# Raw rows and rounded pairs fetched in two tiles each, the first fetches reordered, the last output tiles copied in halves, under a new plan

## Chip, cores and metric

The kernel runs on one core of a Trainium2 chip. The metric is the device time of one execution in microseconds. The kernel before has a median of 574.6 us over three runs (574.01 to 575.79).

## What is computed

Two layers in sequence, for 8 batches of 576 positions: local attention with 8 heads of 64 (a window of 128 and a linear bias), and on its output a mixture of 4 attention experts of which each position uses the best two.

```python
def _attn_ref(q, k, v):
    ...
    scores = scale * np.matmul(q, k.transpose(0, 1, 3, 2))
    ...
    mask = (rel >= 0) & (rel < window)
    scores = np.where(mask, scores + bias[None], -1000000000.0)
    ...
    attn = attn / (np.sum(attn, axis=-1, keepdims=True) + 1e-09)
    return np.matmul(attn, v).astype(np.float32)

def _moe_ref(x, w_gate, wq, wk, wv, wo):
    ...
    logits = x @ w_gate
    topk = np.argpartition(-logits, K, axis=-1)[..., :K]
    ...
    for e in range(E):
        q = x @ wq[e]
        k = x @ wk[e]
        v = x @ wv[e]
        scores = scale * (q @ k.transpose(0, 2, 1))
        causal = np.triu(np.ones((S, S), dtype=bool), 1)
        ...
        ye = a @ v @ wo[e]
        for kk in range(K):
            mask = topk[:, :, kk] == e
            out += mask[..., None] * w[:, :, kk:kk + 1] * ye
    return out.astype(np.float32)
```

## The kernel before

The attention works on 32 groups, a pair of heads of one batch each (`g`, four to a batch). Group `g` goes through scores (`attn_s`: matmuls into tile `s`, mask and bias on VectorE, exponentials on ScalarE into `p`, scaling by 1/sum on GpSimd or ScalarE), transposition by TensorE (`attn_t`, tiles `t`, `pa`) and the product with the values (`attn_pv`, tiles `x`, `xt`, result `xh`, `xl`). After four groups of a batch come its projections (`qkproj`, `vproj`), the experts' scores (`moe_s`, tile `ms`), their transposition (`mt`), the product with the values (`ma`, `mal`) and the output (`moe_wo`, tile `o`, copied to `ot` and stored).

Precise products of f32 numbers are made of rounded ones: a high part and the rest are multiplied apart. For a group the rounded q and k of both heads stand in one tile `h` (two head halves side by side, each with q and a tail of zeros or of the other head, then k), which a DMA on GpSimd's queue fetches and rounds. The raw numbers stand in one tile `r` (q, then k), fetched on SP's queue; `prep` subtracts the rounded from the raw: `q0` and `q1` into `h` itself, `k0` and `k1` into `klA`. There is one buffer of `r`, two of `h`. The first six groups (`N32`) don't use this form: their raw rows, tile `e`, are multiplied as f32; `load_e` fetches the lower 64 partitions on SP and the upper ones on ScalarE's queue (groups 0 to 3) or GpSimd's (groups 4 and 5).

The weights of the projections come in four chunks (`wload`, tile `wst`), are rounded on GpSimd or ScalarE (`wprep`: `WH`) and their rests (`WL`) computed on VectorE or GpSimd. `wo` and the mask table follow.

The order in which instructions stand on each engine is neither the program's nor written by hand: all operations are recorded, and `plan` sorts them by a list schedule. It takes costs of each operation, the longest chain behind it as its rank, offsets of the rank by tile, engine and phase (`off`, 193 numbers in the table `K`), rates for fetches (`dr`), and where an operation may go to one of two engines (`nc.any`), it chooses one. Where TensorE has nothing to do in the plan up to 69.6 us (`f1`), it puts in a matmul of zeros (`warm`, into a tile that nobody reads). Then each engine executes its instructions in that order. SP's and ScalarE's fetches share eight semaphores, so each one waits for the landing of the eighth before it.

Of the kernel before, what the change touches and what calls it, by code (L numbers as in the profile page):

```python
# [417 lines left out]
def attn_moe_kernel(ctx, tc, hd, rd, vd, wall, wo, mk, tb, tm, mt, ident, out):  # L418
# [73 lines left out]
    HW = 2 * QW + 2 * S  # L492
# [8 lines left out]
    def load_e(g):  # L501
        b, p = divmod(g, NP_)
        o1 = QW + S + P
        if g < NP_:
            e = m1.tile([P, 10 * P], F32, tag="mp", name=f"e{g}", bufs=K["mp"])[:, : QW + S]
        else:
            e = p2.tile([P, HW], F32, tag="h", name=f"e{g}")
            for x in range(3):
                nc.alt["hold"][len(nc.ops) + x] = first["w", 1]
            nc.sync.dma_start(e[:, QW + S : o1], hd[b, p, :, QW + S : o1])  # L510
        nc.sync.dma_start(e[:D, : QW + S], hd[b, p, :D, : QW + S])
        q = nc.scalar if g < NP_ else nc.gpsimd
        q.dma_start(e[D:, P : QW + S], hd[b, p, D:, o1 + P : o1 + QW + S])
        raws[g] = e
# [24 lines left out]
    def load_hi(g):  # L539
# [6 lines left out]
        h = p2.tile([P, HW], F32R, tag="h", name=f"h{g}")  # L546
        hh = [h[:, :o1], h[:, o1:]]
# [760 lines left out]
```

## Time and profile before

| | before |
|---|---|
| median of 3 runs | 574.6 us (574.01 to 575.79) |
| profiled execution, its own time | 577.87 us |
| span of the profiled execution | 575.9 us |
| mean granted TensorE clock | 0.996 |
| busy VectorE | 418.0 us (73%) |
| HBM read, written | 65.32 MB, 9.44 MB |

The profile shows one execution. PE is TensorE's matmuls, PEld its weight loads, DVE VectorE, ACT ScalarE, POOL GpSimd; SPq, ACTq and POOLq are the queues on which DMAs are issued. "Idle before" a group is the time in which its engine stood, with what ended it behind the arrow. Every recorded operation is issued from one line (L1220), so instructions are told apart by the tiles that they write and read: `s<-e` writes `s` and reads `e`. Matmuls overlap in the array, so a busy PE may still have small gaps between starts.

### The profile page before, as it was taken

How to read it: one execution, taken by the hardware profiler on the slowest of the kernel's cores; microseconds unless marked ns; L12 is line 12 of the kernel's file. 1: busy time of each engine (PE TensorE's matmuls, PEld its weight loads, DVE VectorE, ACT ScalarE, POOL GpSimd, SP SyncE). 2: the span in 40 equal slices, each digit the busy share in tenths (PEclk: the TensorE clock that was granted, in tenths of full speed). 3: DMA queues.
4: the chain of work that ended last, by engine and by line, in shares of the span. 5: the costliest groups of instructions: out<-in, count | busy, mean ns of one | idle time of the engine just before them, and what ended most of it. 6: DMA issues, size and time to landing. Idle time of an engine off the chain costs nothing.

```text
span 575.9 us, 13867 instructions
## 1 busy us (share of the span) xinstructions
PE 558.8 (97%) x4576; PEld 476.7 (83%) x4576; DVE 418.0 (73%) x1818; ACT 427.6 (74%) x1458; POOL 364.1 (63%) x570
## 2 busy tenths in 40 slices
PE   8799999999999999989999999999999999999996
PEld 7577978888888988979888898888888898898764
DVE  3778779977977789676977689766997668465620
ACT  3776778977797688876888687876789768475863
POOL 3575578686768587675878478695768744063430
PEclk9999999999999999999999999999999999999999
DMA  9934454344452435523453444504455400100013
GB/s 217 304 109 134 153 187 140 129 152 152 170 188 65 148 111 207 189 86 116 160 194 125 136 158 179 207 20 151 153 187 171 147 24 24 73 20 2 1 56 109
DMA packets 24246, 75.64 MB, mean 131 GB/s; under 512 B 2416, under 2 KB 3952, under 8 KB 24176
## 3 DMA queue, kind: packets, MB, share of 16 engines
q1 hardware_dynamic: 16624, 40.72, 22.0%
q0 software_dynamic: 7232, 32.93, 17.5%
q10 hardware_dynamic: 320, 1.11, 0.9%
q8 instruction: 36, 0.59, 0.4%
q14 instruction: 34, 0.28, 0.2%
HBM read 65.32 MB, written 9.44 MB: 130 GB/s over the span
## 4 chain that ended last, share of the span: by engine, by line
PE 74%; DVE 6%; POOL 4%; DMA 4%; ACT 3%; issue 1%; ACTq 0%; POOLq 0%
PE qk L1220 15%; PE s L1220 9%; PE v L1220 8%; PE o L1220 8%; PE ms L1220 6%; PE x L1220 6%; PE mt L1220 6%; PE ma L1220 5%; PE t L1220 5%; DMA r<-in_rd 2%; PE msl L1220 2%; POOL h L1220 2%; DMA h<-in_hd 2%; ACT p L1220 1%; PE mal L1220 1%
## 5 line engine op out<-in xcount | busy, mean ns | idle before, releaser
L1220 ACT ACTIVATE p<-p,nm 128x128 f32<-128x128 f32 x288 | 113.1, 394 | 39.9 <-DVE nm L1220 37.2
L1220 PE MATMUL qk<-xh,WH 128*128 128x288 f32 x512 | 115.4, 308 | 0.0
L1220 POOL TENSOR_TENSOR h<-r,h 64x576 fp32r<-64x576 f32 x52 | 74.0, 1423 | 43.9 <-DMA h<-in_hd 24.3
L1220 POOL TENSOR_SCALAR mp<-mp,mr,w 128x128 f32<-128x128 f32 (+3 forms) x128 | 76.6, 611 | 31.3 <-DVE mr L1220 24.4
L1220 PEld LDWEIGHTS qk<-xh,WH 128*128 128x128 f32 x512 | 82.4, 189 | 5.2 <-issue 1.1
L1220 ACT ACTIVATE mp<-mp,mnm 128x384 f32<-128x384 f32 (+3 forms) x128 | 71.3, 559 | 12.2 <-DVE mnm L1220 10.9
L1220 POOL TENSOR_SCALAR p<-p,r 128x128 f32<-128x128 f32 x156 | 57.2, 380 | 35.7 <-DVE r L1220 29.5
L1220 DVE TENSOR_TENSOR pa<-t,tmt 128x512 f32<-128x512 f32 (+2 forms) x96 | 73.8, 774 | 7.3 <-ACT pa L1220 4.4
L1220 DVE CUSTOM_DVE_ANT_0 mp<-ms,mtt 128x384 f32<-128x384 f32 (+3 forms) x128 | 59.9, 486 | 21.5 <-PE ms L1220 19.9
L1220 POOL TENSOR_TENSOR klA<-r,h 64x576 fp32r<-64x576 f32 x52 | 73.9, 1421 | 2.2
L1220 DVE CUSTOM_DVE_ANT_0 p<-s,tbt 128x128 f32<-128x128 f32 x288 | 71.3, 285 | 2.7 <-PE t L1220 0.8
L1220 PE MATMUL qk<-xh,WL 128*128 128x288 f32 x256 | 71.3, 307 | 0.0
L1220 PE MATMUL s<-h 128*128 128x128 f32 (+2 forms) x260 | 69.2, 286 | 1.9 <-DVE nm L1220 1.9
L1220 PE MATMUL s<-klA,h 128*128 128x128 f32 (+2 forms) x260 | 69.6, 284 | 1.3 <-POOL klA L1220 1.3
L1220 DVE COPY_PREDICATED s<-mkt,s 128x256 f32<-128x256 int32 (+2 forms) x160 | 51.4, 331 | 26.2 <-PE s L1220 24.6
L1220 PE MATMUL v<-WH,xh 128*128 128x260 f32 x288 | 63.1, 298 | 0.1
L1220 PE MATMUL x<-pa,vt 128*64 128x256 f32 (+1 forms) x512 | 62.7, 361 | 0.0
L1220 PE MATMUL t<-idt,p 128*128 128x128 f32 x288 | 56.4, 278 | 5.3 <-ACT p L1220 3.5
L1220 PE MATMUL mt<-idt,mp 128*128 128x128 f32 x320 | 59.2, 274 | 0.1
L1220 ACT COPY mpt<-mt 128x384 f32<-128x384 f32 (+1 forms) x86 | 45.4, 535 | 17.6 <-PE mt L1220 14.1
L1220 ACT ACTIVATION_READ_ACCUMULATOR p<-p,nm 128x1 f32 x288 | 54.2, 188 | 0.0
L1220 PEld LDWEIGHTS s<-h 128*128 128x128 f32 x260 | 48.8, 189 | 5.1 <-issue 2.6
(128 smaller groups left out, 1405.7 us busy)
## 6 DMA issues: line engine op xcount, KB each, us to landing
h<-in_hd POOLq DMA_DIRECT2D x26, 1216.0 KB, 6.6
r<-in_rd SPq DMA_DIRECT2D x26, 576.0 KB, 3.8
vt<-in_vd SPq DMA_DIRECT2D x32, 320.0 KB, 3.0
out<-ot SPq DMA_DIRECT2D x32, 256.0 KB, 2.0
e<-in_hd SPq DMA_DIRECT2D x6, 304.0 KB, 7.8
wst<-in_wall SPq DMA_DIRECT2D x4, 386.0 KB, 6.5
e<-in_hd ACTq DMA_DIRECT2D x4, 272.0 KB, 6.1
out<-ot SPq DMA_DIRECT2D x8, 128.0 KB, 2.4
```

What stands on the lines that cost most here:

```text
L1220: getattr(getattr(tc.nc, e), m)(*a, **k)
```

## The change

`r` becomes `rq` and `rk` (q rows and k rows) with a fetch each, `h` becomes `ha` and `hb` (head 0, head 1) with a fetch each; groups 4 and 5 keep raw rows in `ea` and their tails in `eb`. GpSimd's queue takes the upper halves of groups 1 to 3 from ScalarE's, the second and third of them behind memsets. SP's first fetches stand in another order. The last two output tiles of the last batch are copied half by ScalarE and half by VectorE, and each half is stored by its own queue. All offsets and a few constants of the plan are new: `dr`, the rate of fetches that the planner reckons with in the first 30 us, is 300 in place of 340.

```diff
-K = {'dx': 1200, 'se': 0, 'hd': 1, 'dr': 340, 
...
+K = {'dx': 1200, 'se': 0, 'hd': 1, 'dr': 300, 
...
-            e = p2.tile([P, HW], F32, tag="h", name=f"e{g}")
+            e = p2.tile([P, QW + S], F32, tag="ha", name=f"ea{g}")
+            eb = p2.tile([P, QW + S], F32, tag="hb", name=f"eb{g}")
...
-        q = nc.scalar if g < NP_ else nc.gpsimd
+        if 0 < g < NP_:
+            nc.alt["hold"][len(nc.ops)] = first["z", min(g, 2)]
+        q = nc.gpsimd if g else nc.scalar
...
-            r = raw.tile([P, 2 * S], F32, tag="r", name=f"r{g}")
-            if g < N32 + 2:
-                nc.alt["hold"][len(nc.ops)] = first["w", 1]
-            nc.sync.dma_start(r, rd[b, p])
+            r = [raw.tile([P, S], F32, tag="r" + x, name=f"r{x}{g}") for x in "qk"]
+            for k in range(2):
+                if g < N32 + 2:
+                    nc.alt["hold"][len(nc.ops)] = first["w", 1]
+                nc.sync.dma_start(r[k], rd[b, p, :, S * k : S * k + S])
...
-        h = p2.tile([P, HW], F32R, tag="h", name=f"h{g}")
-        hh = [h[:, :o1], h[:, o1:]]
+        hh = [p2.tile([P, o1], F32R, tag="h" + "ab"[k], name=f"h{'ab'[k]}{g}") for k in range(2)]
...
-        if g < N32 + 2:
-            nc.alt["hold"][len(nc.ops)] = first[g - N32 + K["hd"]]
-        a = hd[b, p]
-        src = bass.AP(tensor=a.tensor, offset=a.offset, ap=[a.ap[0], [o1 + P, 2], [1, o1]])
-        nc.gpsimd.dma_start(h.rearrange("p (a n) -> p a n", a=2), src)
+        for k in range(2):
+            if g < N32 + 2:
+                nc.alt["hold"][len(nc.ops)] = first[g - N32 + K["hd"]]
+            nc.gpsimd.dma_start(hh[k], hd[b, p, :, k * (o1 + P) : k * (o1 + P) + o1])
...
+        if b == B - 1 and t >= NQ - 1:
+            h = DM // 2
+            nc.scalar.copy(ot[:, :h], acc[:, :h])
+            nc.vector.tensor_copy(ot[:, h:], acc[:, h:])
+            for k, q in enumerate((nc.sync, nc.scalar)):
+                n = slice(h * k, h * k + h)
+                if t < NQ:
+                    q.dma_start(out[b, P * t : P * t + P, n], ot[:, n])
+                else:
+                    q.dma_start(out[b - 1, NQ * P :, n], ot[:TAIL, n])
+                    q.dma_start(out[b, NQ * P :, n], ot[TAIL:, n])
+            return
...
     zero()
+    load_e(0)
     nc.sync.dma_start(mkt, mk)
     nc.sync.dma_start(tbt[:, 0], tb[:, 0])
-    load_e(0)
     load_tails()
+    load_e(1)
     nc.sync.dma_start(idt, ident)
-    load_e(1)
```

Three places show what the plan makes of it. In the names, the number behind a tile's name tells its instances apart; `e_112`, `e_114`, `e_119` and `e_120` (`e_122` after the change) are groups 0 to 3, `p_124`, `p_134`, `p_153` the exponentials of groups 0 to 2.

SP's first fetches, before. Ahead of these stand `mkt`, `tbt` and `e_112`.

```order
L1220 DMA tails<-in_hd 128x4x128
L1220 DMA idt<-in_ident 128x128
L1220 DMA e_114<-in_hd 64x1216
L1220 DMA vt_115<-in_vd 128x640
L1220 DMA tmt<-in_tm 128x256
L1220 DMA tbt<-in_tb 128x640
L1220 DMA e_119<-in_hd 64x1216
L1220 DMA vt_116<-in_vd 128x640
L1220 DMA tbt<-in_tb 128x1280
L1220 DMA e_120<-in_hd 64x1216
L1220 DMA wst_121<-in_wall 128x772
L1220 DMA wst_122<-in_wall 128x772
```

SP's first fetches, of the change. Ahead of these stand `e_112`, `mkt` and `tbt`.

```order
L1236 DMA tails<-in_hd 128x4x128
L1236 DMA e_114<-in_hd 64x1216
L1236 DMA idt<-in_ident 128x128
L1236 DMA tbt<-in_tb 128x640
L1236 DMA tmt<-in_tm 128x256
L1236 DMA vt_115<-in_vd 128x640
L1236 DMA e_119<-in_hd 64x1216
L1236 DMA tbt<-in_tb 128x1280
L1236 DMA wst_120<-in_wall 128x772
L1236 DMA vt_116<-in_vd 128x640
L1236 DMA wst_121<-in_wall 128x772
L1236 DMA e_122<-in_hd 64x1216
```

The second weight chunk keeps its place but for one fetch: the lower half of group 3 now stands behind it.

ScalarE around its first rounding of a weight chunk, before.

```order
L1220 COPY pa_140<-t_0_139 128x2x128
L1220 ACTIVATE p_134,sm_97<-p_134,nm_133 128x128 x6
L1220 CAST WH<-wst_122 128x772
L1220 ACTIVATE p_134<-p_134,r_5_148 128x128 x3
L1220 ACTIVATE p_134,sm_97<-p_134,nm_133 128x128
L1220 ACTIVATE p_153,sm_96<-p_153,nm_152 128x128
L1220 CAST xh_149<-x_142 128x512
L1220 ACTIVATE p_134<-p_134,r_0_146 128x128 x4
```

The same place of the change.

```order
L1236 COPY pa_140<-t_0_139 128x2x128
L1236 ACTIVATE p_134,sm_97<-p_134,nm_133 128x128 x5
L1236 CAST WH<-wst_121 128x772
L1236 CAST xh_149<-x_142 128x512
L1236 CAST xh_149<-xt_150 128x64
L1236 ACTIVATE p_134,sm_97<-p_134,nm_133 128x128 x4
L1236 ACTIVATE p_134<-p_134,r_0_146 128x128 x3
L1236 ACTIVATE p_134<-p_134,r_5_148 128x128 x3
```

The rounding moved ahead of four of group 1's nine exponentials; before, one of them stood behind it.

TensorE around the first transposition of group 1 (`t_0_158`), before.

```order
L1220 MATMUL s_1_156<-e_119 128x256
L1220 MATMUL s_4_157<-e_119 128x256
L1220 MATMUL s_0_173<-e_120 128x128
L1220 MATMUL s_3_174<-e_120 128x128
L1220 MATMUL t_0_158<-idt,p_134 128x128 x4
L1220 MATMUL s_0_173<-e_120 128x256
L1220 MATMUL s_3_174<-e_120 128x256
L1220 MATMUL warm_118<-QZm 128x256 x2
L1220 MATMUL s_2_163<-e_119,tails 128x192
L1220 MATMUL warm_118<-QZm 128x256 x2
```

The same place of the change.

```order
L1236 MATMUL s_1_156<-e_119 128x256
L1236 MATMUL s_4_157<-e_119 128x256
L1236 MATMUL warm_118<-QZm 128x256 x12
L1236 MATMUL s_0_154<-e_119 128x128
L1236 MATMUL s_3_155<-e_119 128x128
L1236 MATMUL s_0_154<-e_119 128x256
L1236 MATMUL s_3_155<-e_119 128x256
L1236 MATMUL t_0_158<-idt,p_134 128x128
L1236 MATMUL t_1_160<-idt,p_134 128x128
L1236 MATMUL s_2_163<-e_119,tails 128x192
```

In all, 59 fills (`warm`) stand ahead of that transposition and 41 behind it before; of the change 37 and 24. The order of the last 40 rows of TensorE is the same in both.

## Rows read from the trace of the kernel before

**Rows 1.** The page's first part: busy time of each engine.

```profile
PE 558.8 (97%) x4576; PEld 476.7 (83%) x4576; DVE 418.0 (73%) x1818; ACT 427.6 (74%) x1458; POOL 364.1 (63%) x570
```

**Rows 2.** Busy time by stretch, summed over 72 to 550 us.

```profile
sum 478.00, PE 472.59 PEld 408.39 DVE 365.39 ACT 370.11 POOL 321.66; mean PE 24.87 PEld 21.49 DVE 19.23 ACT 19.48 POOL 16.93
```

**Rows 3.** Fills alone by stretch: PE, PEld busy (count), clock, DMA share, GB/s.

```profile
0.00:8.00 8.00, 6.32 (x29) 6.12 (x29) 1.00 0.80 184
8.00:26.00 18.00, 4.90 (x30) 4.04 (x30) 1.00 1.06 273
26.00:64.00 38.00, 8.05 (x41) 6.30 (x41) 0.96 0.51 164
```

**Rows 4.** Timeline of 0 to 24 us: start, duration, engine, instruction, idle before.

```profile
0.74 2.48 ACTq L1220 DMA_DIRECT2D e<-in_hd  x4
0.74 2.14 POOL L1220 MEMSET KLm<- 64x1152 f32 x2 [0.29 <-POOLq L1293]
...
8.74 1.79 PE L1220 MATMUL s<-e 64*128 64x256 f32 x16 [0.85 <-DMA e<-in_hd]
...
13.41 1.88 PE L1220 MATMUL s<-e 64*128 64x128 f32 x16
...
16.84 0.37 ACT L1220 COPY pa<-t 128x256 f32<-128x256 f32 x1
...
22.90 0.83 ACT L1220 CAST WH<-wst 128x772 fp32r<-128x772 f32 x1 [3.37 <-DMA wst<-in_wall]
```

**Rows 5.** Timeline of TensorE from 20 us.

```profile
26.22 0.73 PE L1220 MATMUL t<-idt,p 128*128 128x128 f32 x4 [3.48 <-ACT p L1220]
```

**Rows 6.** Busy time by stretch, columns PE, PEld, DVE, ACT, POOL, clock, DMA share, GB/s.

```profile
18.00:24.00 6.00, 4.74 (x48) 3.15 (x47) 3.54 (x18) 2.63 (x11) 2.84 (x3) 1.00 1.05 273
28.00:31.40 3.40, 3.40 (x15) 2.33 (x13) 2.72 (x10) 2.50 (x14) 0.83 (x1) 0.50 1.04 361
30.00:72.00 42.00, 41.51 (x343) 33.14 (x343) 33.76 (x145) 29.77 (x120) 26.13 (x40) 0.98 0.41 124
```

**Rows 7.** Waits, and TensorE's at 73.90 us: total in us, times, longest.

```profile
POOL h L1220 <- DMA h<-in_hd: 24.3, 8, 4.9
POOL h L1220 <- DMA r<-in_rd: 16.3, 7, 5.1
...
73.90 0.38 PE L1220 MATMUL s<-klA,h 128*128 128x256 f32 x1 [1.29 <-POOL klA L1220]
```

**Rows 8.** DMA issues: queue, count, KB each, median us to landing.

```profile
h<-in_hd POOLq DMA_DIRECT2D x26, 1216.0 KB, 6.6
r<-in_rd SPq DMA_DIRECT2D x26, 576.0 KB, 3.8
vt<-in_vd SPq DMA_DIRECT2D x32, 320.0 KB, 3.0
out<-ot SPq DMA_DIRECT2D x32, 256.0 KB, 2.0
```

**Rows 9.** GpSimd: two groups of the page's fifth part; DMA issues in its timeline.

```profile
L1220 POOL TENSOR_SCALAR p<-p,r 128x128 f32<-128x128 f32 x156 | 57.2, 380 | 35.7 <-DVE r L1220 29.5
L1220 POOL TENSOR_TENSOR klA<-r,h 64x576 fp32r<-64x576 f32 x52 | 73.9, 1421 | 2.2
...
26.27 1.29 POOL L1220 DMA_DIRECT2D e<-in_hd  x2
364.19 0.78 POOL L1220 DMA_DIRECT2D h<-in_hd  x1
```

**Rows 10.** Waits of the weight loads: the first `ma` of a run.

```profile
PEld ma L1220 <- issue: 7.1, 32, 0.3
```

**Rows 11.** Timeline of the end, from 570.3 us.

```profile
570.38 0.39 PE L1220 MATMUL o<-WOH,ALTm 128*128 128x512 f32 x1
570.62 1.07 ACT L1220 COPY ot<-o 128x512 f32<-128x512 f32 x2 [2.54 <-PE o L1220]
571.24 1.60 SPq L1220 DMA_DIRECT2D out<-ot  x3
```

More of the change, by code (lines that the diff above doesn't have):

```diff
@@ L491, in attn_moe_kernel @@
     QW = S + TAIL
-    HW = 2 * QW + 2 * S
     N32 = K["n32"]
@@ L506, in load_e @@
         else:
-            e = p2.tile([P, HW], F32, tag="h", name=f"e{g}")
+            e = p2.tile([P, QW + S], F32, tag="ha", name=f"ea{g}")
+            eb = p2.tile([P, QW + S], F32, tag="hb", name=f"eb{g}")
             for x in range(3):
                 nc.alt["hold"][len(nc.ops) + x] = first["w", 1]
-            nc.sync.dma_start(e[:, QW + S : o1], hd[b, p, :, QW + S : o1])
+            nc.sync.dma_start(eb[:, :P], hd[b, p, :, QW + S : o1])
+            raws["t", g] = eb[:, :P]
         nc.sync.dma_start(e[:D, : QW + S], hd[b, p, :D, : QW + S])
-        q = nc.scalar if g < NP_ else nc.gpsimd
+        if 0 < g < NP_:
+            nc.alt["hold"][len(nc.ops)] = first["z", min(g, 2)]
+        q = nc.gpsimd if g else nc.scalar
         q.dma_start(e[D:, P : QW + S], hd[b, p, D:, o1 + P : o1 + QW + S])
@@ L528, in load @@
                 load_e(g)
-            r = (raws[g], raws["t"][:, g, :] if g < NP_ else raws[g][:, QW + S : QW + S + P])
+            r = (raws[g], raws["t"][:, g, :] if g < NP_ else raws["t", g])
         else:
-            r = raw.tile([P, 2 * S], F32, tag="r", name=f"r{g}")
-            if g < N32 + 2:
-                nc.alt["hold"][len(nc.ops)] = first["w", 1]
-            nc.sync.dma_start(r, rd[b, p])
+            r = [raw.tile([P, S], F32, tag="r" + x, name=f"r{x}{g}") for x in "qk"]
[3 more added lines that the diff above has]
+                nc.sync.dma_start(r[k], rd[b, p, :, S * k : S * k + S])
         loaded[g] = (r, vt)
@@ L563, in prep @@
             d = slice(D * j, D * j + D)
-            ssub(kl[d, j, lo:hi], r[d, S + lo : S + hi], kh[j][d, lo:hi].bitcast(F32), sube(g))
+            ssub(kl[d, j, lo:hi], r[1][d, lo:hi], kh[j][d, lo:hi].bitcast(F32), sube(g))
             return
         if w == "q0":
-            t, x = qs[0][D:, lo:hi], r[D:, lo:hi]
+            t, x = qs[0][D:, lo:hi], r[0][D:, lo:hi]
         else:
-            t, x = qs[1][:D, TAIL + lo : TAIL + hi], r[:D, lo:hi]
+            t, x = qs[1][:D, TAIL + lo : TAIL + hi], r[0][:D, lo:hi]
         ssub(t, x, t.bitcast(F32), sube(g))
@@ L1046, in zero @@
         nc.vector.memset(QZ.bitcast(F32), 0.0)
+        nc.gpsimd.memset(KL[D:, :, 0, :].bitcast(F32), 0.0)
+        nc.gpsimd.memset(KL[:D, :, 1, :].bitcast(F32), 0.0)
+        first["z", 1] = len(nc.ops) - 1
         for k in range(2):
@@ L1049, in zero @@
             nc.gpsimd.memset(KLA[k][:D, 1, :].bitcast(F32), 0.0)
-        nc.gpsimd.memset(KL[D:, :, 0, :].bitcast(F32), 0.0)
-        nc.gpsimd.memset(KL[:D, :, 1, :].bitcast(F32), 0.0)
+        first["z", 2] = len(nc.ops) - 1
         for k in range(2):
@@ L1168, in attn_moe_kernel @@
     load_hi(0)
+    nc.sync.dma_start(tbt[:, 1], tb[:, 1])
+    nc.sync.dma_start(tmt, tm)
     nc.sync.dma_start(prepped[0][3], vd[0, 0])
     warm()
-    nc.sync.dma_start(tmt, tm)
-    nc.sync.dma_start(tbt[:, 1], tb[:, 1])
     load_e(2)
+    nc.sync.dma_start(tbt[:, 2:], tb[:, 2:])
+    wload(0)
     load_vt(1)
-    nc.sync.dma_start(tbt[:, 2:], tb[:, 2:])
+    wload(1)
     load_e(3)
-    wload(0)
-    wload(1)
     aseq, marks = attn_units()
```

2 lines of the change are left out of this document (1 added, 1 removed).

## The prediction

> **What bounds the kernel now.** I read the page's busy shares first, then busy time by stretch, then the timelines of the first 28 us and of the end, then the waits. TensorE is busy for 97% of the span [rows 1]. From 72 to 550 us it is busy for 472.6 of 478.0 us [rows 2], so that middle part can give back 5.4 us at most unless the matmuls themselves get fewer, and they do not: the order of instructions has the same matmuls before and after, apart from the fills. What is left to win lies ahead of 72 us. There part of TensorE's busy time is fills, which multiply zeros: 29 take the first 8 us, 30 more stand between 8 and 26 us, 41 between 26 and 64 us, 100 in all [rows 3]. The timeline shows what TensorE then waits for [rows 4]. The first score matmul starts at 8.74 us, 0.85 us after the last fill, on the fetch of e; the second group's starts at 13.41 us, on an e whose lower half is SP's sixth fetch. At 22.90 us ScalarE begins its rounding of a weight chunk, after 3.37 us of waiting for that chunk's fetch. Everything queued behind it on ScalarE is late, the scalings of the second group among it, and TensorE stands for 3.48 us until it can transpose them at 26.22 us [rows 5]. From 28.0 to 31.4 us the granted clock is 0.50, the lower of its two levels, right after that wait [rows 6].
>
> The sum below is made against the profiled execution: 577.87 us, of which the span is 575.9. It lies 3.3 us above the median of the runs, 574.6; I carry the difference over to the median.
>
> **First fetches reordered.** SP now issues e of group 0 first and e of group 1 fifth, and ScalarE issues one fetch in place of four (GpSimd has the other three). The first group should start about 8 fills sooner, since 21 stand ahead of it in place of 29, at 6.32/29 = 0.22 us each: 1.7 us [rows 3]. But this is not what sets the end. The weight chunk that ScalarE rounds is, in both orders, a wait that everything behind it shares. Of what stood ahead of that chunk, only the lower half of e of group 3, 304 KB, now comes behind it. At the 273 GB/s that all queues move between 18 and 24 us [rows 6] this is 0.304/273 = 1.1 us. ScalarE's work between the rounding and the first scaling is about as long as before (a rounding, two copies of xh, four exponentials in place of three scalings, two exponentials, a copy). The three fetches that went to GpSimd stand behind one or two memsets there (2.14 us for two [rows 4]); what they delay behind them on GpSimd, more memsets, nobody reads before the scalings of group 0. I take **-1.1 us**. Bounds: 0, if the chunk comes no sooner, and -5.2, if the wait of 3.48 us goes altogether and with it the stretch at half clock (3.4 us, so 1.7 us at the full one).
>
> **Fewer fills behind that wait.** Up to the first transposition of group 1 the order has 59 fills before and 37 now; those are hidden by the fetch either way, so they get no term. Behind it there are 41 before and 24 now. TensorE's weight loads for the 41 take 6.30 us, 0.154 us each [rows 3]; 17 fewer give 2.6 us. Between 30 and 72 us TensorE is idle for 0.5 us only [rows 6]: there the planned gaps were as long as the fills that stand in them, and the new plan is likely to be right about its own as well. I take **-2.6 us**; bounds 0 (waits take the fills' place) and -2.6.
>
> **Raw rows and rounded pairs in two tiles each.** The two halves of a pair's rows can be refetched when their own readers are done. What this can save on the path: TensorE waits once for klA, 1.3 us at 73.9 us; GpSimd waits 24.3 us for h and 16.3 us for r, which costs nothing as long as TensorE does not wait for GpSimd [rows 7]. The table of landings [rows 8] gives 3.0 us for 320 KB and 3.8 us for 576 KB from SP, a line of 2.0 us plus 0.8 us for each 256 KB: half of r should land in 2.9 us. I take the klA wait as gone, **-1.3 us**; bounds 0 and -1.3. [...]
>
> The price is on GpSimd: 26 more issues, and the row of the whole h is 0.78 us, while two issues of 272 KB take 1.29, 0.65 each [rows 9]: 52 x 0.65 - 26 x 0.78 = 13.5 us more of its queue, or 20.3 at 0.78 each. Against this, 24 scalings of p move from GpSimd to ScalarE, 24 x 0.38 = 9.1 us [rows 9]. GpSimd is busy 63% and ScalarE 74% of the span [rows 1], so both are covered by TensorE's own work; if that cover is gone, it is the first rival below. SP gets 26 more issues of some 0.53 us [rows 11] in 576 us, 14 us of a queue that computes nothing: no term.
>
> **The new order of the middle.** TensorE enters a run of 64-column matmuls (x, xt, ma, mal) 66 times before and 70 times now. Such an entry costs 7.1/32 = 0.22 us of idle weight load [rows 10]: 4 x 0.22 = **+0.9 us**; bounds 0 and +1.8 (leaving the run costs the same). Which other waits a new order brings or removes in the middle can't be read from the order; they were 5.4 us in all [rows 2], and I let them stand.
>
> **Last tiles in halves.** The end of TensorE's order is unchanged. Before: last matmul done at 570.77 us, two copies in 1.07 us, three issues in 1.60 us, then the landing of 2.0 us or more [rows 8, 11]. Now each queue again has three issues, SP and ScalarE side by side, and ScalarE's second copy stands behind its first issue: an issue takes 0.53 us on SP here and took 2.48/4 = 0.62 on ScalarE at the start [rows 4], so 0.37 + 0.53 to 0.62 + 0.37 = 1.27 to 1.36 us, where two whole copies took 1.07 [rows 11]. The last issue on SP waits for just that copy. So the halves are paid back by the issue between them: **0**, bounds -0.3 (0.37 + 0.37, if the issue holds nothing up) and +0.3.
>
> **Sum:** -1.1 - 2.6 - 1.3 + 0.9 = **-4.1 us**: 573.8 against the profiled execution, **570.5** against the median.
>
> **The rivals.**
> - *GpSimd pays for the split (slower).* In the middle GpSimd's chain per group is two issues, two subtractions of h, two of klA of 1.4 us each [rows 9], with roundings and scalings between. If the extra issue comes last in that chain, TensorE waits for klA as it did once before, 1.29 us a time [rows 7]. It turns the sign into slower once the six waits eat 4.1 + 1.7 us: five waits too many among 24 groups in the middle. With six, 570.5 + 6 x 1.29 = 578.2. For it: GpSimd already waits 40.6 us for fetches, so it runs late. Against: TensorE waited for it only once. Chance 0.10.
> - *The head is bound by its fetches all through.* Then waits take the place of the 17 fills: 574.6 - 1.1 - 1.3 + 0.9 = 573.1, no change that a measurement can tell. For it: the wait at 22.90 us is a fetch, and the bytes are the same. Against: between 30 and 72 us the DMA engines are busy for under half of the time [rows 6]. Chance 0.22.
> - *The weight chunk comes in time.* The planner now counts on slower fetches (300 in place of 340), so it may have put other work ahead. Then -5.2 - 2.6 - 1.3 + 0.9 = -8.2: 566.4. Against: ScalarE's order has the rounding earlier among the exponentials than before, not later. Chance 0.12.
> - *The halves land no sooner than the whole* (the change then does not do what it says): the klA wait stays, 570.5 + 1.3 = 571.8. [...] Chance 0.08.
>
> **How the numbers follow.** My forecast keeps 0.48. I call 0.3% (1.7 us, about what a measurement of this kernel can tell) no change: 572.9 to 576.3. Faster: 0.44 of the forecast, 0.12, 0.07 of the last rival, 0.08 of the fetch-bound one: 0.71. Same: 0.12 of the fetch-bound one and 0.05 of the rest: 0.17. Slower: GpSimd's 0.10 and 0.02: 0.12. The range goes from 565.5 (the terms at their low ends, -5.2 - 2.6 - 1.3 + 0 - 0.3 = -9.4, give 565.2) to 577.0 (within the first rival); the top of that rival and a little below the third are left out.
>
> **What would show it.** Right: the first score matmul about 2 us sooner; ScalarE's wait for the weight chunk ends 1 us sooner; TensorE's busy time shorter by the 39 missing fills while idle time ahead of 72 us does not grow as much; no wait of TensorE for klA; the stretch from the last matmul to the end as long as before, 5.1 us. Wrong: idle time of TensorE in the middle well above 5.4 us, above all with klA, h or ha as what ended it; or a longer wait at the first transposition of group 1, with a longer stretch at the lower clock behind it; or two such stretches. If the middle loses more than 4 us, the forecast fails whatever the head does.

## The result and the profile after

| | before | changed |
|---|---|---|
| median of the runs, taken in turn on one chip | 575.2 us (574.0 to 577.2, 4 runs) | 581.2 us (580.5 to 582.3, 4 runs) |
| ratio, 95% interval | | 1.0102 [1.0073, 1.0131] |
| profiled execution (span) | 577.87 (575.9) | 582.28 (580.5) |
| TensorE idle, 75 to 550 us | 4.1 us | 6.7 us |
| last matmul to the end of the span | 5.1 us | 5.8 us |

The change makes the kernel 1.0% slower, 6.0 us, where 4.1 us less were forecast; the time lies outside the range. The two profiled executions differ by 4.4 us only, since that of the kernel before lies 2.7 us above its median. The page of the changed kernel opens like that of before [rows 1]:

```profile
span 580.5 us, 13884 instructions
PE 559.9 (96%) x4537; PEld 474.2 (82%) x4537; DVE 418.7 (72%) x1811; ACT 431.0 (74%) x1483; POOL 371.2 (64%) x583
```

TensorE has 39 fewer instructions, just the fills left out, and yet as much busy time and a longer span. So what the fills gave back was spent, and more was lost. Busy time by stretch says where (columns: PE, PEld, DVE, ACT, POOL, each with its count, then clock, DMA share, GB/s). Of the kernel before, then of the changed one:

```profile
75.00:550.00 475.00, 470.88 (x3913) 406.89 (x3914) 364.32 (x1565) 368.18 (x1241) 318.81 (x502) 1.00 0.38 125
```

```profile
11.00:15.00 4.00, 3.85 (x20) 3.23 (x20) 1.91 (x11) 2.74 (x11) 1.06 (x3) 0.57 1.09 268
24.00:32.00 8.00, 6.85 (x30) 5.46 (x30) 6.84 (x41) 6.11 (x27) 2.22 (x5) 0.57 1.05 262
75.00:550.00 475.00, 468.29 (x3879) 402.90 (x3879) 361.85 (x1544) 364.87 (x1250) 320.01 (x510) 1.00 0.43 123
```

In the middle TensorE is idle for 6.7 us in place of 4.1, and 34 matmuls fewer are recorded in the same time. In the head there are now two stretches at a granted clock of 0.57 on the mean, where there was one of 0.50 [rows 6]. Both traces give the clock as 1.00 or 0.50 and as nothing between: in the head it is 0.50 from 28.0 to 31.4 us before, and from 11.3 to 14.7 and from 25.0 to 31.8 us in the changed kernel.

**The head.** The timeline of the changed kernel's first 25 us, against [rows 4, 5]:

```profile
5.55 2.16 PE L1236 MATMUL s<-e 64*128 64x256 f32 x16
7.82 0.29 DVE L1236 CUSTOM_DVE_ANT_0 p<-s,tbt 128x128 f32<-128x128 f32 x1 [0.29 <-DMA tbt<-in_tb]
9.46 0.56 PE L1236 MATMUL s<-e,tails 128*128 128x192 f32 x2 [1.74 <-DVE nm L1236]
21.91 0.83 ACT L1236 CAST WH<-wst 128x772 fp32r<-128x772 f32 x1 [3.70 <-DMA wst<-in_wall]
23.26 0.69 DVE L1236 TENSOR_TENSOR xh<-x,xh 128x512 fp32r<-128x512 f32 x1 [5.24 <-ACT xh L1236]
24.91 0.71 PE L1236 MATMUL s<-e 64*128 64x128 f32 x2 [3.00 <-DVE nm L1236]
```

The first scores start 3.2 us sooner, but TensorE then waits 1.74 us for VectorE's maxima of these scores, ahead of which VectorE itself stood 0.29 us for the bias table. The weight chunk is rounded 1.0 us sooner (21.91 for 22.90), but that is scatter between executions: over the traces of all runs below, the rounding starts at 21.87 to 23.62 us with the old order of the first fetches (six traces, mean 22.54) and at 21.91 to 23.01 us with the new one (eight traces, mean 22.40). What is new is that VectorE's `xh`, which needs ScalarE's work behind that rounding, stands in VectorE's queue ahead of group 1's maxima: VectorE waits 5.24 us, and TensorE 3.00 us behind it. The chunk still sets the head, by another chain. The first transposition of group 1 came at 26.22 us [rows 5] and comes at 27.41 us.

**The middle.** What TensorE waited for between 72 and 560 us (us in total, times, longest):

```profile
PE ms L1236 <- DVE nm L1236: 2.6, 8, 0.4
PE mt L1236 <- ACT mpt L1236: 0.9, 4, 0.2
PE s L1236 <- DVE nm L1236: 0.8, 1, 0.8
PE qk L1236 <- ACT xh L1236: 0.5, 1, 0.5
PE o L1236 <- DVE ALm L1236: 0.5, 2, 0.3
```

The wait for `klA` [rows 7] is gone, as forecast. The first two rows are new, and they come batch after batch: eight waits for the softmax maxima and four for the copy of the transposed mask scores. The timeline around one of the eight, GpSimd, VectorE and TensorE together:

```profile
272.94 1.42 POOL L1236 TENSOR_TENSOR ha<-rq,ha 64x576 fp32r<-64x576 f32 x1
272.90 0.18 DVE L1236 TENSOR_REDUCE ws<-ex 128x5 f32<-128x20 f32 x1 [0.41 <-POOL ex L1236]
273.11 1.28 DVE L1236 TENSOR_SCALAR ws<-ws 128x5 f32<-128x5 f32 x1
274.42 0.19 DVE L1236 RECIPROCAL ws<-ws 128x5 f32<-128x5 f32 x1
274.53 0.28 DVE L1236 COPY_PREDICATED s<-mkt,s 128x128 f32<-128x128 int32 x1
275.26 0.08 DVE L1236 DVE_READ_ACCUMULATOR2_ANT nm<- 128x1 f32 x1
274.83 0.28 PE L1236 MATMUL s<-klA,ha 128*128 128x256 f32 x1
275.50 0.30 PE L1236 MATMUL ms<-KHm,QSm 128*128 128x128 f32 x1 [0.39 <-DVE nm L1236]
```

VectorE adds 1e-9 to 5 numbers a partition, the offset of the gate weights' sum, and takes 1.28 us for it. GpSimd's subtraction of the rounded queries runs from 272.94 to 274.36 us, and the offset ends 0.03 us behind it. Everything behind the offset on VectorE is 1.1 us late, and TensorE stands. The same group of instructions, before and changed (ns min/median/max):

```profile
L1220 DVE TENSOR_SCALAR ws<-ws x8: 171/172/207, 79.0 to 524.2; 128x5 f32<-128x5 f32 x8
```

```profile
L1236 DVE TENSOR_SCALAR ws<-ws x8: 164/738/1318, 87.6 to 532.8; 128x5 f32<-128x5 f32 x8
```

In the order before, none of the eight offsets met a subtraction; in the new one those of batches 2 to 5 start beside one (1.28, 1.28, 1.28, 1.32 us), and that of batch 0 meets the last 0.16 us of one (0.20 us).

**The end**, against [rows 11]:

```profile
574.31 0.40 PE L1236 MATMUL o<-WOH,ALTm 128*128 128x512 f32 x1
574.56 0.37 ACT L1236 COPY ot<-o 128x256 f32<-128x256 f32 x1 [2.65 <-PE o L1236]
574.96 0.42 DVE L1236 COPY ot<-o 128x256 f32<-128x256 f32 x1 [2.72 <-ACT ot L1236]
575.42 0.36 ACTq L1236 DMA_DIRECT2D out<-ot  x1
575.89 0.37 ACT L1236 COPY ot<-o 128x256 f32<-128x256 f32 x1 [0.96 <-DVE ot L1236]
576.30 0.42 DVE L1236 COPY ot<-o 128x256 f32<-128x256 f32 x1 [0.91 <-ACT ot L1236]
576.76 1.19 ACTq L1236 DMA_DIRECT2D out<-ot  x2
```

The half copies don't run side by side. VectorE's half of a tile waits for ScalarE's, though they read different columns. ScalarE's second copy stands behind ScalarE's own issue at 575.42 us, which stores VectorE's first half and so waits for it. The four copies take from 574.56 to 576.72 us, where two whole copies took 1.07 us.

### The profile page after: what moved, and what is told of

Its sections match the earlier page's. It is cut to its first block, busy times and chain, and to the rows that moved or that the text cites. A ratio compares the mean times of both kernels' runs of the same rounds, so it can differ in the third digit from the quotient of the medians.

```text
span 580.5 us, 13884 instructions
## 1 busy us (share of the span) xinstructions
PE 559.9 (96%) x4537; PEld 474.2 (82%) x4537; DVE 418.7 (72%) x1811; ACT 431.0 (74%) x1483; POOL 371.2 (64%) x583
## 4 chain that ended last, share of the span: by engine, by line
PE 64%; DVE 15%; DMA 9%; ACT 8%; issue 2%; POOL 2%; SPq 0%; ACTq 0%; POOLq 0%
PE qk L1236 12%; PE s L1236 8%; PE v L1236 8%; PE o L1236 7%; PE ms L1236 5%; PE mt L1236 5%; PE ma L1236 5%; PE x L1236 4%; ACT p L1236 4%; DVE pa L1236 3%; PE t L1236 3%; DMA ha<-in_hd 3%; DMA tbt<-in_tb 3%; PE msl L1236 3%; DVE p L1236 2%; DVE QSm L1236 2%
## 5 line engine op out<-in xcount | busy, mean ns | idle before, releaser
L1236 ACT ACTIVATE mp<-mp,mnm 128x256 f32<-128x256 f32 (+3 forms) x128 | 71.4, 559 | 11.2 <-DVE mnm L1236 10.3
L1236 DVE COPY_PREDICATED s<-mkt,s 128x256 f32<-128x256 int32 (+2 forms) x160 | 51.4, 330 | 32.7 <-PE s L1236 31.4
L1236 POOL TENSOR_SCALAR p<-p,r 128x128 f32<-128x128 f32 x132 | 47.4, 370 | 31.3 <-DVE r L1236 27.5
L1236 ACT ACTIVATE p<-p,r 128x128 f32<-128x128 f32 x156 | 53.0, 393 | 12.3 <-DVE r L1236 11.1
L1236 PE MATMUL v<-WH,xh 128*128 128x260 f32 x288 | 60.5, 295 | 0.0
L1236 PE MATMUL x<-pa,vt 128*64 128x256 f32 (+1 forms) x512 | 59.7, 357 | 0.6 <-DVE pa L1236 0.6
L1236 ACT COPY mpt<-mt 128x512 f32<-128x512 f32 (+1 forms) x90 | 47.2, 529 | 15.5 <-PE mt L1236 12.7
L1236 PEld LDWEIGHTS x<-pa,vt 128*64 128x64 f32 x512 | 32.9, 137 | 18.8 <-issue 5.3
L1236 PEld LDWEIGHTS mt<-idt,mp 128*128 128x128 f32 x320 | 39.6, 140 | 10.3 <-ACT mpt L1236 2.2
L1236 PEld LDWEIGHTS v<-WH,xh 128*128 128x128 f32 x288 | 45.5, 189 | 1.0 <-issue 0.9
L1236 PE MATMUL ms<-KHm,QSm 128*128 128x384 f32 (+3 forms) x128 | 43.5, 354 | 2.6 <-DVE nm L1236 2.6
```

The lines of the kernel that those rows point to most:

```text
L1236: getattr(getattr(tc.nc, e), m)(*a, **k)
```

## The experiments

The planner sets the order of all engines at once, so a part of the change can't be undone by undoing its lines. The kernels below therefore have the planner's call replaced by a written-out list of instructions, taken from the order of one kernel or the other and carried over to the split tiles (`h` stands for `ha`, `hb`; `r` for `rq`, `rk`); the diffs give each edit in short. x1 to x4, x5 to x8 and x9 to x12 were timed in three rounds on three chips, with the kernel before beside them in each (575.1, 575.2 and 575.1 us), so their medians are compared across rounds; a difference of two medians carries about 1 us. Ratios are against the kernel before. Theory 1: the new order of the middle costs the time. Theory 2: the split fetches cost it.

### x1_split_only: split tiles, everything else as before

```diff
-    seq_ = plan(nc.ops, nc.alt)
+    seq_ = ORDER   # before's order, h -> ha, hb; r -> rq, rk
-        if b == B - 1 and t >= NQ - 1:   # halves of the last tiles
```

> The changed kernel's tiles (raw rows in two, rounded pairs one a head, each fetched alone) issued in the order of the kernel before on every engine, with its first fetches and its whole last tiles. Theory 1 (the new order of the middle costs the time, by some 5 us, the split fetches nothing): within 1.5 us of the kernel before, some 574 to 576 us, with the 1.29 us wait for the low halves of the keys at 74 us gone or shorter. Theory 2 (the split fetches cost it: more issuing on GpSimd and SyncE, smaller transfers): some 579 to 581 us.

573.9 us against 575.1, ratio 0.9981 [0.9960, 1.0002]. TensorE's waits between 72 and 560 us, and four fetches (issues, KB, median us to landing):

```profile
PE t L1376 <- DVE xh L1376: 1.4, 3, 0.5
PE t L1376 <- DVE pa L1376: 0.2, 1, 0.2
```

```profile
ha<-in_hd POOLq DMA_DIRECT2D x26, 608.0 KB, 4.5
hb<-in_hd POOLq DMA_DIRECT2D x26, 608.0 KB, 5.4
rq<-in_rd SPq DMA_DIRECT2D x26, 288.0 KB, 3.2
rk<-in_rd SPq DMA_DIRECT2D x26, 288.0 KB, 2.9
```

The wait for `klA` is gone, and the halves land sooner than the wholes, 4.5 and 5.4 us for 6.6 and 2.9 to 3.2 for 3.8 [rows 8]. Theory 2 falls: the split alone costs nothing, and 1.2 us is about what was forecast for it, though its interval just reaches no change.

A larger wait than that for `klA` is gone too. In the kernel before, on GpSimd, VectorE and TensorE:

```profile
239.85 2.93 POOL L1220 TENSOR_TENSOR h<-r,h 64x576 fp32r<-64x576 f32 x2 [5.12 <-DMA r<-in_rd]
245.74 0.31 DVE L1220 COPY mr<-w 64x1 f32<-64x1 f32 x2 [2.52 <-POOL mp L1220]
247.45 0.30 PE L1220 MATMUL s<-h 128*128 128x128 f32 x1 [1.67 <-DVE nm L1220]
```

GpSimd waits 5.12 us for the fetch of `r`, so its scaling of `mp` is late; VectorE waits for that, and TensorE for VectorE. At the same place of x1 GpSimd waits 4.06 us for `rq`, VectorE 0.42 us, and TensorE not at all.

### x2_whole_tails, x3_after_head, x4_before_head: the new order in pieces

```diff
-        if b == B - 1 and t >= NQ - 1:   # x2: whole last tiles, new order throughout
+    seq_ = AFTER[: gates of batch 0] + BEFORE[gates of batch 0 :]   # x3
+    seq_ = BEFORE[: gates of batch 0] + AFTER[gates of batch 0 :]   # x4
```

> The changed kernel in its own order, with the last two output tiles copied and stored whole as before. Both theories: the end after the last matmul goes from 5.8 to 5.1 us and the rest stays, so 580.5 us against 581.2, since the half copies ran one after another. If the halves cost nothing: 581.2.

> Split tiles, whole last tiles; the changed kernel's order and first fetches up to the gates of batch 0 (74 us), the order of the kernel before from there. Theory 1: the head keeps its 1.5 us and the middle loses nothing, so 573 to 574.5 us, 1 to 2 us below the kernel before. Theory 2: 578 to 580 us.

> Split tiles, whole last tiles; the order and first fetches of the kernel before up to the gates of batch 0, the changed kernel's order from there. Theory 1: the middle loses its 5 us without the head's gain, so 580 to 582 us, and the small waits for VectorE and ScalarE (0.39 and 0.25 us at the first score matmuls of the tails, 0.21 at the transposed masks) stand in each batch as in the changed kernel. Theory 2: like the first of these runs, 579 to 581 us.

x2: 580.7 us, so the new order costs 6.8 us against x1. For the halves 0.5 us are left, less than the medians carry; the two traces show 0.7 us (5.1 us from the last matmul to the end in x2, 5.8 in the changed kernel). x3: 578.1. x4: 582.7. Against x1 the new head alone costs 4.2 us and the new rest alone 8.8, together 6.8: the pieces don't add up, since an order is made for the state that its own head leaves. The joint of x3 shows it, in TensorE's waits and in busy time by stretch:

```profile
PE s L1375 <- DVE nm L1375: 2.7, 2, 2.5
```

```profile
85.00:92.00 7.00, 6.65 (x40) 5.83 (x41) 4.76 (x21) 5.31 (x20) 2.42 (x5) 0.76 0.33 92
```

One wait of 2.5 us up to 85.35 us, which begins 8 us behind the joint, and a granted clock of 0.76 after it: that is most of its 4.2 us, and neither x1 nor x2 has that wait. So x3 doesn't price the head. x4 has the waits that theory 1 names, two waits for GpSimd's `p` of 1.9 us in all that neither x1 nor x2 has, and the offset again at 1.29 us:

```profile
L1376 DVE TENSOR_SCALAR ws<-ws x8: 153/726/1293, 89.2 to 535.4; 128x5 f32<-128x5 f32 x8
```

### x5_ws_later, x8_ws_mpt: the offset moved, and the copy ahead of the scalings

```diff
 # VectorE, batches 2 to 5
-sum, offset, reciprocal of ws; mask of s; two maxima; QSm
+mask of s; two maxima; QSm; sum, offset, reciprocal of ws
 # ScalarE, batches 1 to 4 (x8 alone)
-scaling of p, scaling of p, copy of mpt
+copy of mpt, scaling of p, scaling of p
```

> The changed kernel in its own order with whole last tiles (580.7 us), but in batches 2 to 5 VectorE's sum, offset and reciprocal of the gate weights (ws) stand behind the two softmax maxima and the rounding of qk that followed them. Theory A (in these batches the offset of ws takes 1.28 us in place of 0.17 because it is held while GpSimd subtracts the rounded queries of the next pair, and the two maxima behind it then come late for TensorE, which waits 0.39 and 0.26 us at the mask scores): the 8 waits go, 2.6 us, so about 578 us; the offset may still be held but nobody waits. Rival B (the waits are the order's own, and another late instruction takes their place; or the lost time is in small waits elsewhere): 580 us or more.

> The same, and in batches 1 to 4 ScalarE copies the first transposed mask scores (mpt) ahead of two softmax scalings that it took over from GpSimd, instead of behind them. Theory A: the four waits of 0.21 us at the next mask transposes go as well, 0.9 us, so about 577.2 us. Rival: the scaled probabilities come 0.55 us later, their transposes wait instead, and the time is that of the kernel without this edit.

x5: 583.2 us, 2.4 us above x2: as rival B had it, another late instruction took their place. VectorE, then TensorE, in batch 3:

```profile
274.62 1.05 DVE L1375 TENSOR_SCALAR ws<-ws 128x5 f32<-128x5 f32 x1
275.93 1.23 DVE L1375 TENSOR_TENSOR pa<-t,tmt 128x1024 f32<-128x1024 f32 x1
277.21 1.08 PE L1375 MATMUL x<-pa,vt 128*64 128x256 f32 x8 [1.04 <-DVE pa L1375]
```

The four waits of 0.39 us are gone, as theory A said, and those of 0.26 us stay. But the edit did not do what it was meant to: the offset now meets GpSimd's next subtraction, that of `klA`, takes 1.05 us there, and the masked probabilities behind it are late: four waits of 1.05 us, 4.2 us. A held instruction was moved, not freed, so theory A is still open here. x8: 581.1 us, 2.1 us below x5; the edit on ScalarE is worth more than the 0.9 us of waits that it takes away. Why is not shown.

### x9_no_offset, x10_no_offset_mpt: the offset taken away

```diff
-        nc.vector.tensor_scalar(ws, ws, EPS, None, op0=add)
```

> The changed kernel in its own order with whole last tiles (580.7 us), with VectorE's offset of the gate weights' sum (the addition of 1e-9 to a sum of 1 or more) left out, so that no instruction is held there while GpSimd subtracts. Theory A (the held offset makes the maxima behind it late): VectorE has 1.1 us back in each of batches 2 to 5, the 8 waits at the mask scores (0.39 and 0.26 us) go and no other takes their place, 2.6 us: 578.1 us. Rival B (the order is late anyway; the wait moves to the next instruction, as it moved to the masked probabilities when the offset only changed its place): 580 us or more, with waits of 0.3 to 1 us for VectorE elsewhere in these batches.

> The same, and in batches 1 to 4 the copy of the transposed mask scores ahead of the two scalings that ScalarE took over. Theory A: 0.9 us less for the four waits that show, up to 2 us less by the difference that the same edit made beside the moved offset (583.2 to 581.1): 576 to 577.3 us. Rival: no change against the run without this edit.

x9: 577.5 us, 3.3 us below x2, for leaving out eight instructions of 0.17 us when nothing holds them. x10: 575.9, another 1.6 us. Busy time from 75 to 550 us in x2, x9, x10 and x1:

```profile
75.00:550.00 475.00, 468.74 (x3883) 403.40 (x3883) 363.21 (x1546) 365.42 (x1253) 320.19 (x511) 1.00 0.42 123
```

```profile
75.00:550.00 475.00, 471.02 (x3902) 405.06 (x3901) 360.04 (x1546) 367.81 (x1259) 322.86 (x516) 1.00 0.42 123
```

```profile
75.00:550.00 475.00, 471.35 (x3911) 406.07 (x3911) 361.02 (x1549) 368.44 (x1262) 323.41 (x517) 1.00 0.42 123
```

```profile
75.00:550.00 475.00, 472.85 (x3933) 408.71 (x3932) 364.45 (x1563) 369.56 (x1246) 326.38 (x526) 1.00 0.39 124
```

TensorE's idle time goes from 6.3 to 4.0, 3.7 and 2.1 us. Theory A holds and rival B falls: no other wait of that size took the place. Two edits that leave every matmul where the new plan put it take back 4.9 of the 6.8 us between x2 and x1.

The traces can also be split at the gates of batch 0 (the start of VectorE's first comparison of the router's outputs, `G`):

| | before | x1 | changed | x2 | x9 | x10 |
|---|---|---|---|---|---|---|
| gates of batch 0, us | 75.6 | 74.4 | 74.1 | 74.2 | 73.1 | 74.2 |
| from there to the end of the last matmul, us | 495.1 | 492.6 | 500.6 | 500.0 | 496.6 | 495.6 |

Behind the gates x2 takes 7.4 us more than x1. x9 takes 3.3 of them back and x10 1.1 more, near the 0.9 us of waits that its edit removes; 3.0 us are left. Ahead of the gates, x2, x9 and x10 have one order and differ by 1.2 us all the same: executions vary there by that much, so the 1.6 us between the medians of x9 and x10 is not to be read more finely. Another VectorE TENSOR_SCALAR, `cnt<-cnt`, is held once in batch 1 of x2, x9 and x10 (1.06, 1.23 and 1.07 us), and no wait of TensorE stands near it.

### x6_first_fetches, x7_fewer_fills: two terms of the forecast alone

```diff
 # x6: x1, with the changed kernel's first fetches, their queues, GpSimd's memsets
 # x7: x1, fills behind the first transposition of group 1
-2 2 1 3 1 7 4 4 7 5 3 2
+1 1 1 2 0 4 2 2 4 4 2 1
```

> Split tiles, whole last tiles and the compute order and fills of the kernel before (573.9 us), with the changed kernel's order of the first fetches, their queues and the order of GpSimd's memsets. The forecast's first term (the weight chunk that ScalarE rounds lands about 1 us sooner and the 3.5 us wait behind it shrinks by as much): 572.8 us. Rival (what comes sooner is paid by what comes later, as the bias table and the upper halves of the next groups): 574 us or more.

> Split tiles, whole last tiles and the compute order of the kernel before (573.9 us), with the fills behind the first transposition of group 1 cut from 41 to 24, run by run as the changed kernel has them in number. The forecast's second term (each fill stands on TensorE's path, 0.154 us): 2.6 us less, 571.3 us. Rival (the fills stand where TensorE would wait for a softmax or a weight anyway): 573.5 to 574.5 us, the gaps in their place.

x6: 574.1 us, 0.2 above x1, ratio 0.9981 [0.9957, 1.0006]. In x6's timeline the chunk comes no sooner than in x1 (22.64 for 22.05 us), and TensorE now waits for another fetch, `e`, ahead of group 1's transposition:

```profile
22.64 0.83 ACT L1376 CAST WH<-wst 128x772 fp32r<-128x772 f32 x1 [4.81 <-DMA wst<-in_wall]
24.20 0.58 PE L1376 MATMUL s<-e 64*128 64x128 f32 x4 [2.77 <-DMA e<-in_hd]
```

The rival holds, as far as medians tell: what comes sooner is paid by what comes later. x7: 572.9 us, 1.0 below x1, ratio 0.9943 [0.9919, 0.9967]: faster than the kernel before. Of the 2.6 us, about 1.0 is real; in the traces the gates of batch 0 come at 73.2 us, for 74.4 in x1. From 30 to 72 us x7 shows:

```profile
30.00:72.00 42.00, 40.70 (x333) 32.14 (x331) 33.56 (x148) 30.29 (x120) 29.60 (x46) 1.00 0.48 142
```

TensorE is now idle for 1.3 us there, where it was for 0.5 [rows 6]: part of the fills stood in waits.

### x11_no_fills_behind, x12_trimmed: how far that goes

```diff
 # x11: no fills behind the first transposition of group 1 (59 in all)
 # x12: 37 ahead of it, 24 behind (61 in all)
-out tile 7_4 copied on ScalarE
+out tile 7_4 copied on VectorE (x12)
```

> Split tiles, whole last tiles, the compute order of the kernel before, and none of the 41 fills behind the first transposition of group 1. By the gain of the first 17 (573.9 to 572.9, 0.06 us each) the other 24 give 1.4 us: 571.5 us. Rival (a second stretch of half clock, since TensorE has gaps there in their place): a granted clock of 0.5 again between 34 and 60 us, and 573.5 to 576 us.

> Split tiles, the compute order of the kernel before, fills cut to 37 ahead of the first transposition of group 1 and 24 behind it (the changed kernel's numbers), and the last output tile copied whole on VectorE while ScalarE copies the one before it whole. Expected: the fills ahead stand where TensorE waits for fetches, so nothing from them (or a second half-clock stretch ahead of 24 us, which costs nothing either, since the first groups wait for their fetches); 0.3 to 0.5 us from the two copies side by side: 572.3 to 572.7 us. If fills ahead count as those behind did (0.06 us each): 571.2 us.

x11: 572.9 us, as x7. Busy time by stretch:

```profile
26.00:34.00 8.00, 8.00 (x47) 4.76 (x46) 6.41 (x36) 6.24 (x30) 4.02 (x5) 0.63 0.94 299
34.00:60.00 26.00, 23.17 (x185) 16.33 (x184) 21.41 (x87) 18.44 (x74) 17.20 (x27) 1.00 0.39 119
```

No second half-clock stretch, so the rival falls; but 2.8 us of idle time from 34 to 60 us: the last 24 fills cover waits and cost nothing. x12: 572.3 us, ratio 0.9951 [0.9930, 0.9972], the lowest median of the study, 1.5% below the changed kernel; against x7 and x11 it is within what the runs can tell. Its end:

```profile
565.88 0.59 ACT L1375 COPY ot<-o 128x512 f32<-128x512 f32 x1 [2.54 <-PE o L1375]
566.06 0.69 DVE L1375 COPY ot<-o 128x512 f32<-128x512 f32 x1 [2.47 <-PE o L1375]
566.49 1.55 SPq L1375 DMA_DIRECT2D out<-ot  x3
```

Two tiles of their own are copied side by side. It brings less than 0.1 us (4.87 us from the last matmul to the end, 4.94 in x1): the three issues behind, 1.55 us on SP, are what ends last.

## Why the prediction was wrong

| term | forecast, us | measured, us | by |
|---|---|---|---|
| first fetches reordered | -1.1 | +0.2 | x6 - x1 |
| fewer fills behind the wait | -2.6 | -1.0 | x7 - x1 |
| raw rows and rounded pairs split | -1.3 | -1.2 | x1 - before |
| new order | +0.9 | +7.6 | (x2 - x1) less the two first rows |
| last tiles in halves | 0 | +0.5 | changed - x2 |
| sum | -4.1 | +6.1 | changed - before: +6.0 |

Each row carries about 1 us, so +0.2 and +0.5 mean "about nothing". That the rows add up follows from how they are formed.

**The new order of the middle is the step that failed.** It was priced at four entries into 64-column runs, +0.9 us, and of all other waits the text said "I let them stand". They didn't: the new order cost 7.6 us by the medians, and 7.4 by the traces, all behind the gates of batch 0. Of these, 3.3 are the held offset (x9), and 1.6, or 1.1 by the traces, the copy of `mpt` behind two scalings on ScalarE, which has 24 more scalings than before (x10). I had counted those 24 as covered, from ScalarE's busy share, without asking who stands behind each on its queue. The rest is not pinned down, and its cause stays open. In the traces x10 is 3.0 us longer than x1 behind the gates of batch 0. Half of that is idle time, in single waits of up to 0.6 us for ScalarE, VectorE and GpSimd; for the other half no run here tells a cause, and the four entries may be part of it. The sentence "If the middle loses more than 4 us, the forecast fails whatever the head does" held.

**Fewer fills: right in sign, too large.** "There the planned gaps were as long as the fills that stand in them" took the whole 0.154 us for each. Measured, the first 17 give 0.06 us each and the next 24 nothing. In the changed kernel little of it is seen, since its own head has new waits in their place (1.74 and 3.00 us for VectorE): its gates of batch 0 come 0.3 us ahead of x1's, where the two terms of the head promised 3.7 us.

**First fetches: the chunk came no sooner.** The term reckoned with 304 KB less ahead of the chunk. That the two profiled executions differ by 1.0 us, for 1.1 worked out, is luck: x2, with the changed kernel's fetches and order, has the chunk at 22.82 us, x1, with those of the kernel before, at 22.05, and x6 shows no gain in its time. The step also took ScalarE's chain behind the chunk as the only one. VectorE's `xh` hangs on it too, and now stands ahead of group 1's maxima: the first transposition of group 1 starts at 25.2 to 26.9 us in the seven traces with the old order of the compute instructions, and at 27.1 to 28.3 in the seven with the new one. The rival "The head is bound by its fetches all through" is the one that came true in the head. I had named "two such stretches" at half clock as a sign against me, and two there are (11 to 15 and 24 to 32 us, 0.57 each). They can't be priced from these runs: the profile of x2, the same order, has only the second, and its gates of batch 0 come at the same time (74.2 and 74.1 us).

**The split: right in sign, its size partly luck.** The `klA` wait went and halves land sooner, so the rival "The halves land no sooner than the whole" fell. But the step priced one wait where two went. GpSimd's waits for `r` were said to cost nothing "as long as TensorE does not wait for GpSimd"; at 247.45 us they cost the kernel before 1.67 us by way of VectorE. The traced execution lies 2.7 us above the median, and how much of this wait the others have is not known. The rival that GpSimd pays for the split did not come true by its own mechanism: no wait for `klA` came back. But part of the slower time hangs on GpSimd's subtractions, through an instruction of VectorE that reads none of their data.

**The halves: mis-sized, 0 for +0.5.** The step took ScalarE's second copy to wait for the issue ahead of it alone, 1.27 to 1.36 us from the start of the first copy to the end of the second. That issue waits for VectorE's half, which waits for ScalarE's: it took 1.70 us, and VectorE's last half ended 0.46 us later. The two halves of a tile share the accumulator that they read and the output tile that they write, and no run tells which of the two makes one wait. What the traces have is that VectorE's two waits (2.72 and 0.91 us) were both ended by ScalarE's copy, and that in x12, with two tiles, the copies overlap by 0.41 us.

## What to carry to other kernels

When a planner or a changed cost reorders everything, the new order can be the largest term of the change, whatever the edit was: bound it by what stands behind what on each in-order queue, not by the idle time that the old order had. Look in the trace for short instructions that take longer beside another engine's long one: here a VectorE TENSOR_SCALAR of 0.17 us took 1.28 to 1.32 us where it started beside a GpSimd subtraction of 1.42 us. Removing the held one helped (3.3 us, x9), and moving it only moved the wait (x5); moving what holds it was not tried. Transfer the old order onto the new structure before judging either: here the structure was worth about 1 us and the order cost more than all of it.

## What the runs showed of the hardware

- Two VectorE TENSOR_SCALARs, `ws<-ws` and `cnt<-cnt`, were held where they started while GpSimd ran a TENSOR_TENSOR on 64x576 elements (1.42 us), and ended about 0.03 us after it (0.028 to 0.032 us in the five cases of `ws<-ws` in the changed kernel's trace). `ws<-ws`, 0.17 us when alone, took 1.28 to 1.32 us beside the subtraction of the queries (12 cases in three kernels) and 1.05 to 1.08 beside that of `klA` (8 cases in x5 and x8). `cnt<-cnt`, 0.17 us when alone, took 0.71 to 1.23 us beside the subtraction of the queries (5 cases), and 0.18 where it started 0.13 us ahead of one (x8).
- Beside GpSimd's scaling of `p` (0.38 us), `cnt<-cnt` took 0.22 us and ended 0.03 us after it when it started 0.17 us into it (28 cases in seven traces, four of them in the changed kernel's), and its usual 0.17 us when it started 0.05 us into it (24 cases in six traces). Why VectorE is held there no run shows.
- Reductions, reciprocals, masks, maxima and copies on VectorE in the same stretches took what they take elsewhere. In the changed kernel's trace the medians inside a subtraction and apart from all of them are 0.16 and 0.16 us for the sums `r<-sm` (128x8), 0.18 and 0.17 for the reciprocals `mr`, 0.30 and 0.29 for the masks `s` (128x128), 0.29 and 0.29 for the maxima `p<-s`, 0.16 and 0.16 for the copies `lg`; the sum of `ws` has a median of 0.17 to 0.18 us in the traces of the kernel before, the changed one, x1, x2, x4 and x9. The comparison `Q<-lg`, 0.23 us elsewhere, took 0.35 to 0.72 us beside a subtraction in seven traces (0.38 in the changed kernel's, at 73.74 us).
- The fetches of half the bytes in x1 took, against the whole ones of the kernel before, 68% and 82% of the landing time (`ha` 4.5 and `hb` 5.4 of 6.6 us, 608 KB for 1216) and about 80% (`rq` 3.2 and `rk` 2.9 of 3.8 us, 288 KB for 576).
